# Products of the identity in TensorE's planned pauses, six places for the last loads of u, and another order of the work

## The chip, the cores and the metric

The kernel runs on one core of one Trainium2 chip. The metric is the device time of one execution in microseconds (us). TensorE (PE) multiplies into the eight banks of PSUM, VectorE (DVE) and ScalarE (ACT) empty the banks and do the elementwise work, GpSimd (POOL) does reductions over partitions and some copies, and SyncE (SP) issues nearly all transfers. A multiply of float32 numbers that must keep their accuracy is written as three multiplies of rounded parts (high times high, high times low, low times high).

## The reference

```python
def reference(q, k, v, moe_*, moe2_*):
    # attention: batch 4, 8 heads, 576 tokens, 64 numbers a head; heads 0-3 see a window of 32,
    # heads 4-7 every fourth token of a window of 128
    attn = softmax(where(mask, q @ k.T / 8, -1e9)) @ v          # -> x (4, 576, 512)
    # first feed-forward part: 512 -> 1024 -> 512, gated by a convolution over 3 tokens
    h = relu(x @ w_in); gate = sigmoid(conv3(h, conv_w))
    x = (h * gate) @ w_out
    # second part: Fourier transform over tokens and numbers, real part, then layer norm and 512 -> 2048 -> 512
    u = x + real(fft(fft(x, axis=1), axis=2))
    un = (u - mean(u)) / sqrt(var(u) + 1e-6)
    return u + relu(un @ w_ch1) @ w_ch2
```

## The kernel before

The stages follow one another and overlap: the attention of the four batches (`tick`: scores, maximum, exponential, product with v, transposes; 14 ticks a batch), the first feed-forward part batch by batch (`m1`, `m2`), the Fourier transform as products with tables (`dft`), the layer norm (`ln`), and the second feed-forward part. The last is done first in three `runs` over eight blocks of 128 hidden rows (`n1`, `n2`), and then over the pairs of blocks that are left, for three sets of six token tiles (`pair7`, `down6`; 16 steps k = 0 to 15, the last set of tokens in k = 12 to 15). Its sums stay in six PSUM banks over the steps of a set. At the end of a set `add_up` loads for each tile the residual u from DRAM, adds the bank to it on DVE and stores the result. In the three runs the partial sums go back to DRAM in the same way. The loads of u go to places that a `Ring` hands out in turn. From step k = 7 that ring has four places, so the fifth and the sixth load of a set use the first two again. The weights come in as float64 and are narrowed and split on DVE (`Weights.narrow`: three instructions; `Weights.split`: a subtraction and a copy).

No engine's instructions are written out in the order in which they run. Each piece of work is given to `Plan.add` with its engines, its assumed duration and what it reads and writes. `Plan.urgency` works out a due time (`key`) for each. `NUDGES` is a list of seeds: each seed draws a stretch of due times and moves the due times in it at random by up to 1, 2, 4 or 8 us. `Plan.order` then plays the engines through in planned time and picks, for each engine when it comes free, the ready work of lowest due time. It lists the work in that order, and `Plan.issue` emits the instructions; each engine then runs its own part of the list strictly from the top, waiting for semaphores. The planned times themselves don't reach the chip, only the order does. The plan's duration for a product is that of one clock of TensorE throughout:

```python
        if b.form.dtype == F32R:
            us = max(0.109, 0.014 + 0.000417 * n)
...
        else:
            us = 0.014 + 0.0004 * n
```

The line L270 of the profile is the call of `matmul` or `transpose` in `Plan.products`, L257 that of all elementwise work in `Plan.run`, L299 that of a transfer in `Plan.dma`; L639 and L642 are the normalising of attention on DVE and ACT. The rows that matter here name tiles: `pb` is a PSUM bank, `wf` a pair of weight blocks, `hid` the hidden layer, `x` the tokens of one batch or the place that later holds weights, `rows` a scratch tile of which `cv_t`, `g_t` and `hpad` are parts, `ud` the DRAM copy of u, `raw` the place of incoming float64 weights (later of u and of results), `xb` the normalised attention output before its transpose with `ident`, and `tb` the Fourier tables.

Of the kernel before, what the change touches and what calls it, by code (L numbers as in the profile page):

```python
# [12 lines left out]
F32 = mybir.dt.float32  # L13
# [4 lines left out]
BF16 = mybir.dt.bfloat16  # L18
# [6 lines left out]
DM, FF1, FF2 = 512, 1024, 2048  # L25
# [90 lines left out]
class View:  # L116
# [3 lines left out]
    def __init__(self, tile_, form, ops=()):  # L120
        self.tile, self.form, self.ops = tile_, form, ops
# [65 lines left out]
class Work:  # L187
# [2 lines left out]


NUDGES = (72966, 90854, 53149, 44608, 8896, 40657, 44910, 40292, 90802, 9591, 97362, 78696,
          82639, 89740, 72233, 58905, 68874, 57268, 11083, 9893, 22435, 84083, 88604, 81921,
          11822, 6492, 54663, 30756, 71614, 11936, 95714, 64261, 51939,)


LAT = {"PE": 0.25, "DVE": 0.12, "ACT": 0.15, "POOL": 0.2, "SP": 0.0, "NO": 0.0}
# [5 lines left out]
class Plan:  # L203
    def __init__(self, engines):
        self.engines, self.works, self.key, self.piece = engines, [], 1e9, None
        self.opened = []


    def touch(self, w, view, write):
# [14 lines left out]
        keep.append((w.id, write, box))  # L224
        s.log = keep

    def add(self, where, fn, reads, writes, key=None, nbytes=0, after=()):
        w = Work()
        w.id = len(self.works)
        w.where, w.fn, w.deps, w.bytes, w.after = where, fn, set(after), nbytes, {}  # L230
        w.key = self.key if key is None else key
        self.works.append(w)
        for v in reads:
            self.touch(w, v, False)
        for v in writes:
            self.touch(w, v, True)
        return w

    def run(self, where, op_, key=None, **kw):
# [20 lines left out]
    @contextmanager  # L260
    def products(self, key):

        self.piece = []
        yield self
        todo, self.piece = self.piece, None
        us = sum(t[0] for t in todo)

        def fn(_):
            for _, name, a, kw in todo:
                getattr(self.engines["PE"], name)(*[v.real() for v in a], **kw)  # L270
        self.add({"PE": us}, fn, [v for t in todo for v in t[2][1:]], [t[2][0] for t in todo], key)

    def mm(self, o, a, b, start, stop, more=False):
        n = b.n()
# [35 lines left out]
    def order(self):  # L310
        W = self.works
        for w in W:
            w.succ, w.left, w.ready, w.start = [], len(w.deps), 0.0, None
        for w in W:
            for d in w.deps:
                W[d].succ.append(w.id)
        self.urgency()
        for seed in NUDGES:
            rng = random.Random(seed)
            a = rng.uniform(0, 560)  # L320
            z = a + rng.uniform(4, 50)
            amp = rng.choice((1, 2, 4, 8))
            for w in W:
                if a < w.key < z:
                    w.key += rng.uniform(-amp, amp)
        self.urgency()
        free = dict.fromkeys(("PE", "DVE", "ACT", "POOL", "SP", "NO"), 0.0)
        can = {e: {} for e in free}
        bus, drift = 0.0, 0.0
        out = []  # L330

        def can_wait(w, end):
            return w.key < 1e8 and end < w.key + min(w.where.values()) + drift

        def offer(w):
            for e in w.where:
                can[e][w.id] = w
        for w in W:
            if not w.left:
                offer(w)  # L340
        while any(can.values()):
            best = None
            for e, c in can.items():
                if c:
                    t = max(free[e], min(w.ready for w in c.values()))
                    if best is None or t < best[0]:
                        best = t, e
            t, e = best
            pick = None

            wait = WAIT.get(e, 0.0)
            for w in sorted((w for w in can[e].values() if w.ready <= t + wait + 1e-9), key=lambda w: w.key):
                late = False
                for e2, us in w.where.items():
                    if e2 != e:
                        queue = sum(x.where[e2] for x in can[e2].values()
                                    if x.key < w.key and x.ready <= t and len(x.where) == 1)
                        if max(free[e2], t) + queue + us < t + w.where[e] - 1e-9 and not (
                                us < w.where[e] and can_wait(w, t + w.where[e] + 0.5)):
                            late = True  # L360
                if not late:
                    pick = w
                    break
            if pick is None:

                free[e] = min([f for x, f in free.items() if f > t + 1e-9] + [t + 0.3])
                continue
            w = pick
            for x in w.where:
                del can[x][w.id]  # L370
            t = max(t, w.ready)
            w.start, w.eng = t, e
            if e == "PE":
                drift += 0.1 * (t - w.key - drift)
            end = t + w.where[e]
            free[e] = end
            if w.bytes:
                begin = max(bus, end)
                bus = begin + w.bytes / 265e3
                end = bus + 2.0  # L380
            out.append(w)
            for s in w.succ:
                x = W[s]
                lat = 0.0 if w.bytes else LAT[e] if e not in x.where else 0.0
                x.ready = max(x.ready, end + lat)
                x.left -= 1
                if not x.left:
                    offer(x)
        assert len(out) == len(W), [w.id for w in W if w.start is None][:5]
        return out  # L390

    def issue(self):
# [4 lines left out]
class Pool:  # L397
# [28 lines left out]
    def fill(self, n):  # L426

        if n % LINE:
            self.tile([128, n % LINE // 4], F32, "room")
# [12 lines left out]
def tile_kernel(ctx: ExitStack, tc: tile.TileContext, forms, qt_in, ktp, ktd, vtp, vtd, wm1, wm2, conv_w,  # L442
                tab, mask, ident16_in, ident_in, out):
    nc = tc.nc
    ctx.enter_context(tc.manual_schedule())
    P = Plan({"ACT": nc.scalar, "DVE": nc.vector, "POOL": nc.gpsimd, "PE": nc.tensor, "SP": nc.sync})
# [18 lines left out]
    def dve(op_, us, key=None, **kw):  # L465
        P.run({"DVE": us}, op_, key, **kw)
# [27 lines left out]
    ident = const.tile([128, 128], F32, "ident")  # L494
# [523 lines left out]
    hidden, rings, later_, tmp7, tok = {}, {}, [], [], {}  # L1018
# [115 lines left out]
    def sums7(j, raw, place_):  # L1134

        a, b = (r.bitcast(F32) for r in raw)
        for x, w in ((a, W2.tiles[0, 2 * j]), (b, W2.tiles[0, 2 * j + 1])):
            w = w.bitcast(F32)
            dve("tensor_tensor", on_dve(512), out=x[:, 0:512], in0=w[:, 0], in1=w[:, 1], op=ALU.add)
        x11, x12, s1, s2 = (a[:, 256 * i:256 * i + 256] for i in range(4))  # L1140
        x21, x22, s3, s4 = (b[:, 256 * i:256 * i + 256] for i in range(4))
        for o, x, y, op in ((s1, x21, x22, ALU.add), (s2, s1, x11, ALU.subtract),
                            (s3, x11, x21, ALU.subtract), (s4, x12, s2, ALU.subtract)):
            dve("tensor_tensor", on_dve(256), out=o, in0=x, in1=y, op=op)
        for i, r in enumerate((a, b)):
            o = place_[:, 2 * i:2 * i + 2]
            v = r[:, 512:1024].rearrange("p (i n) -> p i n", i=2)
            copy(o[:, :, 0], v, ("ACT", "POOL"))
            lo_of(o[:, :, 1], v, o[:, :, 0])
# [81 lines left out]
                add_up(SIX[s][t], acc, at + step * (t + 1) / 6, True, 2 if end and t == 5 else 1)  # L1231


    dve("memset", 0.05, out=tiny)
    P.add({"DVE": 0.05}, lambda _: nc.vector.memset(eps.real(), 1e-9), [], [eps], -95)

# [50 lines left out]
    for k in range(2 * NF1):  # L1287
        _, i, f = W1.todo[k]
# [59 lines left out]
    def stage(j):  # L1348
        return comb[:, 7 * (j % 2):7 * (j % 2) + 7]
# [10 lines left out]
    at = T5  # L1360
    for r, (p, _) in enumerate(runs):
        nt = len(SETS[p])
        for f in range(R0):
            step = WHEN["first"][1] if r == 0 else 1.38 * nt
            if r == 0:
                at = WHEN["first"][0] + step * f
            if (r, f) == (1, 0):
                at = T5
# [4 lines left out]
            if (r, f) == (1, 1):  # L1373
# [11 lines left out]
                flat = [g.rearrange("p j l n -> p (j l n)") for g in groups]  # L1385
# [20 lines left out]
    todo = [(0, j) for j in range(R0 // 2)] + [(s, j) for s in range(3) for j in late]  # L1406
    tokens7(0, tok[0])
    free = [r.bitcast(F32)[:, DM * i:DM * i + DM] for r in raws for i in range(2)]
    left = iter(range(R0 + 6, NF2))
    for k, (s, j) in enumerate(todo):  # L1410
        if k == 7:
            rings["u"], rings["o"] = Ring(rings["u"].views[:2] + free[:2]), Ring(rings["o"].views[:2] + free[2:])
        if j == late[1] and s < 2:
            tokens7(s + 1, tok[s + 1])
        hid = hid_t if k % 2 else other[k >= 4]
        pair7(s, j, hid, tok[s], comb, ring, sums, at, STEP)
        if k < 2:
            sums7(k + 2, (few(), few()), part(k))
        for _, f in zip(range(3 if k < 2 else 1), left):
            second7(f, few)  # L1420
        down6(s, j, hid, at + STEP, STEP, bool(j == 0 or s and j == late[0]), j == late[-1], s == 2)
        if 2 <= k < 6:
            weights7(k + 2, few, stage(k))
        at += STEP
# [80 lines left out]
```

## Time and profile before

| | before |
|---|---|
| median of 3 runs | 747.86 us (745.51 to 748.53) |
| time of the profiled execution | 749.69 us |
| its span, first to last instruction | 747.9 us |
| TensorE busy with products | 724.0 us, 97% |
| VectorE busy | 561.5 us, 75% |
| ScalarE, GpSimd busy | 344.4 us, 152.4 us |
| mean granted TensorE clock | 0.982 |

A busy share says how long an engine had an instruction in work; it says nothing on what it waited for in the rest. The granted clock is 1 at 2.4 GHz and 0.5 at 1.2 GHz, and a TensorE at the lower clock is as busy as at the higher one while it does half the work. What a stretch of a stage is worth is therefore read from three things together: TensorE's pauses, its clock, and which engine was working without a pause at that time.

### The profile page before, as it was taken

The page shows a single profiled execution, that of the slowest core. Times are in us where ns is not written, and L with a number is a line of the kernel's source. Part 1 is how long each engine was busy: PE and PEld are TensorE (multiplying, and loading weights), DVE is VectorE, ACT ScalarE, POOL GpSimd, SP SyncE. Part 2 cuts the span into 40 slices and gives each one's busy share as a digit, 9 for nine tenths or more (in the row PEclk, how much of TensorE's full clock was granted, in tenths as well). Part 3 has the DMA queues.
Part 4 walks back from the last instruction along what each step waited for, and adds up shares of the span by engine and source line. Part 5 has one row for each costly group of instructions (what it writes and reads, how often), then busy time and mean ns, then how long its engine had stood idle before and what let it go on. Part 6 is the DMA issues. An engine that isn't in the chain of part 4 may idle for free.

```text
span 747.9 us, 11906 instructions
## 1 busy us (share of the span) xinstructions
PE 724.0 (97%) x4189; PEld 642.6 (86%) x4189; DVE 561.5 (75%) x1189; ACT 344.4 (46%) x891; POOL 152.4 (20%) x168
## 2 busy tenths in 40 slices
PE   7899989999999999998999999999999999999997
PEld 5788879998998999886888888899999889988895
DVE  6889999899989689889788889576878738324223
ACT  4768767766676565463243325233233323222220
POOL 4646514443555112110000100010011000000000
PEclk9869999999999999999899999999999999999999
DMA  9944454323510834686966914133545799648303
GB/s 251 258 130 136 163 152 136 100 74 116 185 51 29 288 131 127 208 273 225 314 236 227 301 46 132 29 140 113 156 156 186 247 351 325 180 118 277 90 1 112
DMA packets 75095, 126.57 MB, mean 169 GB/s; under 512 B 7570, under 2 KB 35986, under 8 KB 74396
## 3 DMA queue, kind: packets, MB, share of 16 engines
q1 hardware_dynamic: 74236, 122.86, 51.9%
q0 software_dynamic: 432, 2.67, 0.9%
q8 instruction: 33, 0.54, 0.3%
q10 hardware_dynamic: 368, 0.28, 0.1%
q14 instruction: 26, 0.21, 0.1%
HBM read 89.85 MB, written 35.94 MB: 168 GB/s over the span
## 4 chain that ended last, share of the span: by engine, by line
PE 80%; DVE 9%; DMA 5%; ACT 3%; POOL 1%; issue 1%; SPq 1%; ACTq 0%; DVEq 0%; POOLq 0%
PE pb L270 80%; DMA maskt<-in_mask_dram 2%; DVE rows L257 2%; POOL mx L257 1%; DMA ud<-y 1%; DVE sm L257 1%; DVE sq L257 1%; DVE wf L257 1%; SPq L299 1%; DVE win L257 1%; DMA KT<-in_ktd_dram 1%; DVE y L257 1%; DMA rows<-ud 1%; DVE hid L257 1%; DVE raw L257 1%
## 5 line engine op out<-in xcount | busy, mean ns | idle before, releaser
L270 PE MATMUL pb<-wf,hid 128*128 128x512 f32 x870 | 230.6, 400 | 2.5 <-DVE hid L257 2.5
L270 PEld LDWEIGHTS pb<-wf,hid 128*128 128x128 f32 x870 | 158.5, 190 | 29.3 <-DVE hid L257 3.0
L270 PE MATMUL pb<-x,wf 128*128 128x288 f32 x768 | 115.7, 301 | 2.1 <-ACT rows L257 1.2
L270 PEld LDWEIGHTS pb<-x,wf 128*128 128x128 f32 x768 | 107.6, 190 | 5.6 <-ACT rows L257 2.1
L257 POOL PARTITION_ALL_REDUCE mx<-sm x56 | 88.0, 1586 | 78.0 <-DVE sm L257 42.4
L270 PE MATMUL pb<-wf,wc 128*128 128x384 f32 (+1 forms) x414 | 85.2, 343 | 0.0
L257 DVE TENSOR_TENSOR work<-pb,work 128x384 f32<-128x384 f32 x48 | 26.7, 556 | 71.1 <-ACT work L257 38.2
L270 PEld LDWEIGHTS pb<-wf,wc 128*128 128x128 f32 x414 | 74.2, 188 | 5.9
L257 ACT COPY work<-pb 128x384 f32<-128x384 f32 x48 | 23.0, 479 | 88.1 <-PE pb L270 88.1
L257 DVE SCALAR_TENSOR_TENSOR rows<-rows,convw 128x576 f32<-128x576 f32 x64 | 54.7, 855 | 4.1 <-ACT rows L257 3.3
L270 PE MATMUL pb<-wf 128*128 128x512 f32 x216 | 55.1, 393 | 0.0
L270 PEld LDWEIGHTS pb<-VT,sm 104*72 104x72 f32 (+1 forms) x448 | 41.9, 162 | 8.4 <-ACT sm L257 4.8
L270 PE MATMUL pb<-VT,sm 104*72 104x65 f32 (+1 forms) x448 | 44.3, 246 | 4.7 <-ACT sm L257 1.9
L642 ACT ACTIVATE xb<-pb,rs 72x64 f32<-72x64 f32 (+1 forms) x196 | 44.4, 306 | 4.3 <-DVE rs L257 4.1
L270 PEld LDWEIGHTS pb<-wf 128*128 128x128 f32 x216 | 40.1, 188 | 6.6
L270 PE MATMUL pb<-QT,KT 128*104 128x144 f32 (+1 forms) x224 | 42.6, 314 | 0.7 <-DMA QT<-in_qt_dram 0.6
L257 ACT ACTIVATE rows<-pb 128x288 f32<-128x288 f32 x64 | 26.3, 411 | 34.4 <-PE pb L270 33.2
L270 PE MATMUL pb<-wf,wf 128*128 128x512 f32 (+1 forms) x162 | 39.9, 386 | 0.0
L270 PEld LDWEIGHTS pb<-QT,KT 128*104 128x104 f32 (+1 forms) x224 | 34.2, 184 | 6.6 <-issue 3.6
L257 DVE TENSOR_TENSOR sm<-sm,mx 104x288 f32<-104x288 f32 (+1 forms) x56 | 33.8, 606 | 7.2 <-POOL mx L257 7.1
L257 ACT ACTIVATE hid<-pb 128x512 fp32r<-128x512 f32 (+1 forms) x32 | 18.3, 572 | 42.7 <-PE pb L270 42.5
L270 PEld LDWEIGHTS pb<-wf,wf 128*128 128x128 f32 x162 | 29.8, 188 | 5.5
(193 smaller groups left out, 1224.2 us busy)
## 6 DMA issues: line engine op xcount, KB each, us to landing
raw<-in_wm_dram SPq DMA_DIRECT2D x42, 512.0 KB, 5.0
wc<-cd SPq DMA_DIRECT2D x56, 256.0 KB, 2.9
cd<-wc SPq DMA_DIRECT2D x4, 1792.0 KB, 10.9
rows<-ud SPq DMA_DIRECT2D x24, 256.0 KB, 2.7
y<-yd SPq DMA_DIRECT2D x18, 256.0 KB, 3.1
ud<-y SPq DMA_DIRECT2D x18, 256.0 KB, 4.6
wf<-nd SPq DMA_DIRECT2D x18, 256.0 KB, 4.2
QT<-in_qt_dram SPq DMA_DIRECT2D x31, 144.0 KB, 3.7
```

The source lines that it names most:

```text
L257: getattr(self.engines[eng], name)(**a)
L270: getattr(self.engines["PE"], name)(*[v.real() for v in a], **kw)
L299: self.engines[eng].dma_start(out=out.real() if outs else out, in_=in_.real() if ins else in_)
L642: nc.scalar.mul(out=x[:, i], in_=p[:, i], mul=r[:, i:i + 1])
```

## The change

There are three parts.

1. `Plan.order` notes when TensorE has been left without work for over 0.4 us of planned time (after the first 8 us of the plan). Ahead of the work that ends such a pause it puts multiplications of the identity: `fill` looks for a bank whose uses so far have all ended in the plan and whose next use begins a new sum, and `busy_with` issues n plain bf16 products of 128 x 128 by 256 columns into it, n so that they end 0.25 us before the planned start of that work, at 0.12 us each. Nothing reads what they write. The plan's own times aren't changed by them.
2. From step k = 12 on the ring for u has six places, in the tile `flat[3]` (weights that were last used in step 3), and that for the results six as well, two of `rows` and four of `raw`.
3. `NUDGES` loses four seeds (81921, 6492, 54663, 71614) and gains 21.

```diff
@@ NUDGES
-          82639, ..., 88604, 81921,
-          11822, 6492, 54663, 30756, 71614, 11936, 95714, 64261, 51939,)
+          82639, ..., 88604, 11822,
+          30756, 11936, 95714, 64261, 51939, 63844, 16121, 48697, 73536, 40816, 51048, 85030,
+          41210, 53495, 13473, 46513, 14900, 32254, 45147, 44590, 28542, 77181, 66469, 2489,
+          13351, 95203,)
@@ Plan.add
+        for t in {v.tile for v in (*reads, *writes) if v.tile.whole}:
+            self.uses.setdefault(t, []).append((w, t in fresh))
@@ Plan.products
+        fresh = {}
+        for _, _, a, kw in todo:
+            fresh.setdefault(a[0].tile, kw.get("start", True))
@@ Plan.order
+        seen = dict.fromkeys(self.uses, (0, 0.0))
+        def fill(t0, t1):
+            free_at = []
+            for tile_, uses in self.uses.items():
+                i, end = seen[tile_]
+                while i < len(uses) and uses[i][0].start is not None:
+                    x = uses[i][0]
+                    i, end = i + 1, max(end, x.start + x.where[x.eng])
+                seen[tile_] = i, end
+                if 0 < i < len(uses) and uses[i][1]:
+                    free_at.append((end, len(free_at), tile_))
+            end, _, tile_ = min(free_at, default=(t1, 0, None))
+            n = int((t1 - max(t0, end) - 0.25) / 0.12)
+            return self.busy_with(tile_, max(t0, end), n) if n > 0 else []
...
             if e == "PE":
+                if 8.0 < t and t - last > 0.4 and self.busy_with:
+                    out += fill(last, t)
+                last = t + w.where[e]
@@ tile_kernel
+    def busy_with(tile_, at, n):
+        w = Work()
+        w.where, w.eng, w.start, w.bytes, w.deps, w.key, w.ready, w.id = {"PE": 0.12 * n}, "PE", at, 0, set(), at, at, -1
+        def fn(_):
+            x = ident.real().bitcast(BF16)
+            for _ in range(n):
+                nc.tensor.matmul(tile_.real[:, 0:256], x[:, 0:128], x, start=True, stop=True)
+        w.fn = fn
+        return [w]
+    P.busy_with = busy_with
@@ the steps of the last part
+        if k == 12:
+            rings["u"] = Ring([flat[3].bitcast(F32)[:, DM * i:DM * i + DM] for i in range(6)])
+            rings["o"] = Ring(rings["o"].views[:2] + free)
```

## Rows read from the trace of the kernel before

**Rows 1.** The page: busy times, and the chain that ended last by engine.
```profile
PE 724.0 (97%) x4189; PEld 642.6 (86%) x4189; DVE 561.5 (75%) x1189; ACT 344.4 (46%) x891; POOL 152.4 (20%) x168
...
PE 80%; DVE 9%; DMA 5%; ACT 3%; POOL 1%; issue 1%; SPq 1%; ACTq 0%; DVEq 0%; POOLq 0%
```

**Rows 2.** Busy time by stretch: stretch, length, engines, granted clock, DMA share, GB/s.
```profile
0.00:8.00 8.00, 6.03 (x23) 3.21 (x24) 4.70 (x15) 1.87 (x3) 0.95 (x6) 1.00 0.77 209
8.00:58.00 50.00, 42.49 (x318) 39.08 (x317) 40.47 (x91) 36.18 (x125) 29.62 (x23) 0.83 0.78 211
58.00:108.00 50.00, 46.76 (x343) 42.30 (x343) 47.78 (x92) 36.92 (x110) 23.05 (x22) 1.00 0.51 156
108.00:300.00 192.00, 190.96 (x1320) 175.18 (x1319) 170.21 (x361) 125.42 (x360) 77.68 (x88) 1.00 0.38 123
300.00:348.00 48.00, 46.59 (x256) 39.87 (x256) 43.12 (x111) 23.40 (x48) 6.18 (x10) 1.00 0.72 239
348.00:353.50 5.50, 1.98 (x13) 1.21 (x11) 5.43 (x13) 2.88 (x5) 0.91 (x1) 0.92 0.67 184
353.50:742.80 389.30, 389.24 (x1925) 341.70 (x1925) 249.02 (x510) 117.78 (x244) 14.05 (x21) 0.99 0.55 179
742.80:747.90 5.10, 0.00 (x0) 0.00 (x0) 0.75 (x2) 0.00 (x0) 0.00 (x0) 0.73 0.45 167
```

**Rows 3.** The same columns for the stretches around the lower clock.
```profile
13.00:17.60 4.60, 2.48 (x24) 1.99 (x23) 3.15 (x9) 3.96 (x16) 3.12 (x3) 1.00 1.03 288
18.50:21.70 3.20, 3.20 (x20) 3.19 (x19) 1.98 (x4) 1.62 (x5) 2.31 (x2) 0.53 1.04 244
33.00:35.40 2.40, 0.97 (x9) 0.55 (x7) 2.25 (x8) 1.66 (x9) 0.33 (x1) 0.94 0.98 292
35.40:40.40 5.00, 2.90 (x21) 2.54 (x21) 4.33 (x16) 3.49 (x14) 2.83 (x2) 0.50 0.83 235
40.40:48.70 8.30, 7.72 (x37) 7.34 (x37) 6.37 (x12) 5.02 (x17) 4.32 (x3) 0.50 0.37 113
...
352.20:359.70 7.50, 6.23 (x15) 4.94 (x16) 7.13 (x14) 1.46 (x3) 0.00 (x0) 0.54 1.01 291
```

**Rows 4.** The chain that ended last, from 352 us: start, length, what.
```profile
353.47 385.20 PE pb L270 x1907
...
738.69 0.70 DVE rows L257
...
739.79 4.18 DMA rows<-ud
```

**Rows 5.** DVE's timeline at the end; in brackets, the idle before and its releaser.
```profile
740.05 0.69 DVE L257 TENSOR_TENSOR raw<-raw,pb 128x512 f32<-128x512 f32 x1 [0.67 <-PE pb L270]
741.41 0.69 DVE L257 TENSOR_TENSOR rows<-rows,pb 128x512 f32<-128x512 f32 x1 [0.67 <-PE pb L270]
744.17 0.75 DVE L257 TENSOR_TENSOR rows<-rows,pb 128x256 f32<-128x256 f32 x2 [2.07 <-DMA rows<-ud]
```

**Rows 6.** TensorE's timeline: a plain bf16 product at the higher clock, and its successor.
```profile
6.88 0.33 PE L270 MATMUL pb<-maskt,ident 128*128 128x384 bf16 x1
7.04 0.81 PE L270 MATMUL pb<-QT,KT 128*128 128x192 f32 x4
```

**Rows 7.** TensorE's timeline: work that ended a pause, the first, a middle and last.
```profile
13.74 0.89 PE L270 MATMUL pb<-VT,sm 128*96 128x65 f32 x8 [0.51 <-ACT sm L257]
...
35.76 0.50 PE L270 MATMUL pb<-ident,xb 72*128 72x72 f32 x2 [0.68 <-ACT xb L642]
...
353.47 4.64 PE L270 MATMUL pb<-wf,hid 128*128 128x512 f32 x10 [2.51 <-DVE hid L257]
```

**Rows 8.** Timeline after the long pause: the last weights' split, and their first product.
```profile
358.72 0.68 DVE L257 TENSOR_TENSOR x<-rows,x 128x512 fp32r<-128x512 f32 x1
359.69 0.69 DVE L257 TENSOR_TENSOR x<-rows,x 128x512 fp32r<-128x512 f32 x1 [0.29 <-ACT x L257]
...
361.36 1.52 PE L270 MATMUL pb<-x,hid 128*128 128x512 f32 x6
```

More of the change, by code (lines that the diff above doesn't have):

```diff
@@ L192 @@
 NUDGES = (72966, 90854, 53149, 44608, 8896, 40657, 44910, 40292, 90802, 9591, 97362, 78696,
-          82639, 89740, 72233, 58905, 68874, 57268, 11083, 9893, 22435, 84083, 88604, 81921,
-          11822, 6492, 54663, 30756, 71614, 11936, 95714, 64261, 51939,)
[4 rows of a table added]
 LAT = {"PE": 0.25, "DVE": 0.12, "ACT": 0.15, "POOL": 0.2, "SP": 0.0, "NO": 0.0}
@@ L206, in __init__ @@
         self.opened = []
+        self.uses, self.busy_with = {}, None
     def touch(self, w, view, write):
@@ L225, in touch, with add @@
         s.log = keep
-    def add(self, where, fn, reads, writes, key=None, nbytes=0, after=()):
+    def add(self, where, fn, reads, writes, key=None, nbytes=0, after=(), fresh=()):
         w = Work()
@@ L270, in fn @@
                 getattr(self.engines["PE"], name)(*[v.real() for v in a], **kw)
-        self.add({"PE": us}, fn, [v for t in todo for v in t[2][1:]], [t[2][0] for t in todo], key)
+        fresh = {}
+        for _, _, a, kw in todo:
+            fresh.setdefault(a[0].tile, kw.get("start", True))
+        self.add({"PE": us}, fn, [v for t in todo for v in t[2][1:]], [t[2][0] for t in todo], key,
+                 fresh=[t for t, new in fresh.items() if new])
     def mm(self, o, a, b, start, stop, more=False):
@@ L328, in order @@
         can = {e: {} for e in free}
-        bus, drift = 0.0, 0.0
+        bus, drift, last = 0.0, 0.0, 0.0
         out = []
+        seen = dict.fromkeys(self.uses, (0, 0.0))
[12 more added lines that the diff above has]
+            return self.busy_with(tile_, max(t0, end), n) if n > 0 else []
         def can_wait(w, end):
@@ L388, in order @@
                     offer(x)
-        assert len(out) == len(W), [w.id for w in W if w.start is None][:5]
+        assert all(w.start is not None for w in W), [w.id for w in W if w.start is None][:5]
         return out
```

1 row of the table NUDGES is left out of this document.

## The prediction

> **What bounds the kernel now.** I read the page first [rows 1]: TensorE is busy 97% and makes up 80% of the chain that ended last. A share of 97% leaves little to fill, so the next question is where the rest lies. The table by stretches [rows 2] answers it. From 353.5 to 742.8 us TensorE has no pause at all (389.24 of 389.30 us): half of the run is bound by TensorE alone, at 2.4 GHz but for its first six microseconds. Before that it pauses for 2.0 us until 8 us, 7.5 us from 8 to 58, 3.2 us from 58 to 108, 1.0 us from 108 to 300, 1.4 us from 300 to 348 and 3.5 us from 348 to 353.5; then there are 5.1 us at the end. In the three stretches with pauses after 58 us VectorE has no room: 47.78 of 50, 43.12 of 48, 5.43 of 5.5 us. So there VectorE sets the pace, and between them TensorE does.
>
> The same table with narrower stretches shows the second loss [rows 3]. Three times TensorE ran at 1.2 GHz: for 3.2 us from 18.5, for 13.3 us from 35.4 and for 7.5 us from 352.2. Each time it had been broken up before: busy for 2.48 of 4.60 us ahead of the first, 0.97 of 2.40 ahead of the second, and the longest pause of the run (2.51 us [rows 7]) led into the third. The work in these stretches is 3.20, 2.90 + 7.72 and 6.23 us; at 2.4 GHz it takes half, so the whole price of the lower clock is (3.20 + 10.62 + 6.23) / 2 = 10.0 us, of which 6.9 us lie before 50 us. Whether it is paid at the end is another matter. Up to 40 us the DMA share is 0.83 to 1.04: transfers, not TensorE, set the pace there.
>
> Last, the chain from 352 us on [rows 4]: one unbroken piece of TensorE to 738.7, then an addition on DVE, then a load of u of 4.18 us that could be issued only when that addition had read the place it goes to.
>
> **The change part by part.**
>
> **Six places for u.** The additions of the last set start 1.36 us apart (740.05, 741.41), each when TensorE has finished its bank; the sixth starts at 744.17, after 2.07 us of idle time that ended with the load [rows 5]. With a place of its own its load doesn't wait for an addition, and the tile that it goes to was last read hundreds of microseconds earlier. The addition then starts at 741.41 + 1.36 = 742.77, **1.40 us** earlier, and the two stores behind it move with it. The loads are the same six in number and bytes, so nothing is added to the queue; issued earlier, they lie beside 389 us without a pause of TensorE. Bounds: -1.4 us if nothing else moves, 0 if the six loads are issued as late as now. I take -1.4, since the row shows exactly one cause.
>
> **The filling, its price.** A plain product of 384 bf16 columns is followed 0.16 us later by the next [rows 6]: 0.417 ns a column, so 256 columns take 0.107 us, and 0.213 us at half the clock. How many there will be depends on the plan's pauses, which no row shows; as an estimate I take the trace's own. After 8 us and before the last product there are 18 pauses over 0.4 us, 14.9 us in all, the first of 0.51 and the last of 2.51 us [rows 7]. By the rule of the change (length less 0.25, over 0.12, rounded down) they hold 78 products, 8.3 us at full clock. In a real pause they cost nothing; TensorE waits anyway. Where the plan has a pause and the chip none, they cost their full length. Bounds: 0 and +8.3 us. The plan's durations know one clock; the chip's TensorE is late by up to 6.9 us early on, which shifts all later work with it, so most pauses should still be there. I take +1.0, an eighth. The weights of these products are loaded from the identity, which came in with the first transfers, and the bank chosen is the one longest free, so I take no new wait from them.
>
> **The filling, the clock before 50 us.** If the pauses around 13 to 17 and 33 to 40 us are filled but for some 0.3 us each, TensorE is busy for roughly three quarters of these stretches in place of 2.48 of 4.60 and 0.97 of 2.40 us, and it has stayed at 2.4 GHz through 58 to 108 us with pauses like these. Bounds: 0 and -6.9 us. Of this the first 1.6 us and the part to 40.4 us (1.5 us) lie under full transfer queues. The 7.72 us after 40.4 are the part that can count: 3.9 us. VectorE is busy 6.37 of 8.30 us there, so it can follow by at most 1.9 us before it is the bound, and it stays the bound to 108 us. I take **-1.8**.
>
> [...]
>
> **The filling, the clock after 352 us.** The six microseconds of work would take 3.1 us less, and after them TensorE doesn't pause again, so what is won is kept. But VectorE is busy 7.13 of 7.50 us, and the weights whose first product starts at 361.36 are ready at 360.38 [rows 8]: with the order unchanged TensorE could be 0.98 us earlier and no more. Bounds: 0 and -3.1. I take **-1.2**, near the row.
>
> **The new order.** Drawn from the seeds themselves, the added ones move due times from 48 to 423 us of the plan, eight of them within 86 to 140; the removed ones moved 38 to 80 and 187 to 210. It neither adds nor takes away work. What it can win is at most the pauses after 58 us, 3.2 + 1.0 + 1.4 + 3.5 = 9.1 us [rows 2]. VectorE has 22 us to spare from 108 to 300, so a weight conversion put off from before 108 would give room. Losing is as easy: another crowding of VectorE like that at 348 costs 3.5 us, two cost 7. Bounds: -9.1 and +7. I take **-2.5**, a good quarter of what is there, between the ends and nearer to the pauses that exist than to those that would have to appear.
>
> **Sum.** -1.4 + 1.0 - 1.8 - 1.2 - 2.5 = -5.9 us. Against the profiled execution (749.69 us, of which 747.9 are the span and 1.8 lie around it) that is 743.8. The median of the three runs is 747.86, 1.83 lower; there the sum gives **742.0 us**, -0.8%. Differences of up to 0.5% (3.7 us) are what a measurement here can't tell from none.
>
> **The rivals.**
>
> *Everything meets.* The order closes the pauses of VectorE's stretches and the clock holds: -1.4 - 3.5 - 3.1 - 6 = -14, 734 us. For it speaks that these are the places where pauses lie; against it, that VectorE is busy over 90% in each, so its work must go elsewhere, not only in another order.
>
> *VectorE takes it back.* TensorE gains before 50 and after 352 us, and waits for VectorE instead; only the end is left: 747.86 - 1.4 = 746.5. VectorE's 47.78 of 50 us speak for it, its spare 22 us later against it.
>
> *The clock falls anyway.* The quarter of a microsecond left open in each pause, or pauses in other places than planned, leave TensorE as broken up as before. Then the two clock terms vanish and 742.0 + 3.0 = 745.0 remain. For it speaks that TensorE was still busy over half of the time ahead of the first fall; against it, the 2.4 GHz held through 58 to 108 us.
>
> *The filling stands in the way* (slower). TensorE comes to the products after their pause has passed, and ready work queues behind them, with what waits for its banks on ACT and DVE. If all 78 meet no pause: +8.3 - 1.4 = +6.9, 754.8 us. At 13 products (1.4 / 0.107) the gain of the end is gone if nothing else is won, at 48 the kernel is slower by over 0.5%. For it: TensorE runs up to 6.9 us behind a plan that knows one clock. Against it: the pauses are waits for ACT, DVE and transfers, which move along with TensorE.
> The Trainium skill (TensorE: Matmul & The Clock Gate, Part 3, "What overlaps and what doesn't") has matmuls start and end strictly in program order; no row here shows one overtaking another, and by this rule such a filling can't be passed.
>
> **How the numbers follow.** The forecast, 738 to 745 us, gets 0.40; everything meets 0.15; VectorE takes it back 0.16; the clock falls anyway 0.15; the filling stands in the way 0.14. Faster by over 0.5% is below 744.1 us: 0.37 of the first case, all 0.15 of the second, 0.03 of the fourth: 0.55. Slower by over 0.5%, above 751.6: 0.12, nearly all of the last. The rest, 0.33, is in between. For 8 in 10 the range starts at 735 (a third of the second case is left out below) and ends at 750 (0.13 above).
>
> **What would show it.** After the change the sixth addition follows the fifth by about 1.4 us and no load of u lies in the chain's end. Bf16 products of 256 columns stand in TensorE's timeline between 8 and 360 us, about 78. The granted clock is 1.00 at 18 to 22 and 40 to 49 us and after the pause near 350. TensorE's pauses after 58 us add up to about 6.5 us. The prediction is wrong if the filling lengthens stretches that had no pause, if VectorE's crowded stretches grow, or if pauses appear after 353 us.

## The result, and the profile after

The changed kernel takes 740.63 us (median of 7 runs, 738.23 to 743.23) beside 747.39 us of the kernel before (7 runs, 745.51 to 748.57): a ratio of 0.9907, 95% interval 0.9883 to 0.9931, or 6.9 us less, give or take 1.8. Run again for the experiments, beside 18 runs of the kernel before, it gave 739.00 and 0.9889 (0.9866 to 0.9913). The forecast was 742.0 us in 735 to 750, and faster.

Busy times, granted clock by slices of a fortieth of the span, and the chain that ended last by engine, from the page of the changed kernel:

```profile
PE 728.4 (98%) x4312; PEld 647.8 (88%) x4312; DVE 557.1 (75%) x1187; ACT 350.1 (47%) x903; POOL 148.0 (20%) x158
...
PEclk9989999999999999999999999999999999999999
...
PE 86%; DMA 6%; DVE 5%; ACT 1%; POOL 1%; SPq 0%; issue 0%; ACTq 0%; DVEq 0%; POOLq 0%
```

TensorE has 123 products more and its share rose, although the kernel computes nothing more; the products of the identity count as busy. So the first line of this page has become useless as a measure of how well TensorE is used. The table by stretches, in the columns of [rows 2], and the group of the new products by shape:

```profile
8.00:58.00 50.00, 45.95 (x392) 42.20 (x390) 42.49 (x95) 38.12 (x132) 31.46 (x24) 0.93 0.85 228
58.00:108.00 50.00, 48.95 (x361) 44.53 (x360) 47.22 (x92) 37.53 (x112) 23.12 (x20) 1.00 0.47 147
108.00:300.00 192.00, 191.22 (x1331) 176.37 (x1329) 170.28 (x375) 126.83 (x357) 74.65 (x84) 1.00 0.40 130
300.00:348.00 48.00, 48.00 (x286) 41.26 (x286) 43.33 (x104) 26.23 (x52) 5.84 (x10) 1.00 0.70 232
348.00:353.50 5.50, 5.50 (x26) 4.57 (x25) 5.43 (x11) 2.03 (x4) 0.00 (x0) 1.00 0.97 281
353.50:736.00 382.50, 382.41 (x1907) 335.88 (x1905) 242.90 (x499) 117.62 (x246) 12.31 (x17) 1.00 0.54 178
736.00:739.90 3.90, 0.12 (x1) 0.00 (x0) 0.75 (x2) 0.00 (x0) 0.00 (x0) 0.94 0.37 134
```

```profile
L1271 PE MATMUL pb<-ident 128*128 128x256 bf16 x123 | 17.3, 285 | 0.0
```

Three things differ from [rows 2 and 3]. The clock is 0.93 in place of 0.83 from 8 to 58 us, and 1.00 from 300 to 736 us; the 5.50 us from 348 are full where TensorE was busy for 1.98. The last stretch, behind TensorE's last products, is 3.9 us long where it was 5.1. VectorE's additions at the end:

```profile
734.80 0.69 DVE L262 TENSOR_TENSOR raw<-wf,pb 128x512 f32<-128x512 f32 x1 [0.67 <-PE pb L275]
736.16 0.75 DVE L262 TENSOR_TENSOR raw<-wf,pb 128x256 f32<-128x256 f32 x2 [0.67 <-PE pb L275]
```

The sixth follows the fifth by 1.36 us and waits for TensorE alone; in [rows 5] it followed by 2.76 and waited for its load.

### The profile page after: what moved, and what is told of

Its sections match the earlier page's. It is cut to its first block, busy times and chain, and to the rows that moved or that the text cites. A ratio compares the mean times of both kernels' runs of the same rounds, so it can differ in the third digit from the quotient of the medians.

```text
span 739.9 us, 12155 instructions
## 1 busy us (share of the span) xinstructions
PE 728.4 (98%) x4312; PEld 647.8 (88%) x4312; DVE 557.1 (75%) x1187; ACT 350.1 (47%) x903; POOL 148.0 (20%) x158
## 4 chain that ended last, share of the span: by engine, by line
PE 86%; DMA 6%; DVE 5%; ACT 1%; POOL 1%; SPq 0%; issue 0%; ACTq 0%; DVEq 0%; POOLq 0%
PE pb L275 85%; DMA raw<-in_wm_dram 3%; DMA QT<-in_qt_dram 2%; DVE win L262 1%; PE pb L1271 1%; POOL mx L262 1%; DMA maskt<-in_mask_dram 1%; DVE sm L262 1%; DVE raw L262 1%; DVE rows L262 0%; SPq L308 0%; DVE wc L262 0%; DVE hid L262 0%; DVE fo L262 0%; DVE x L262 0%
## 5 line engine op out<-in xcount | busy, mean ns | idle before, releaser
L275 PE MATMUL pb<-x,wf 128*128 128x288 f32 x768 | 113.9, 298 | 0.5 <-ACT rows L262 0.5
L275 PEld LDWEIGHTS pb<-x,wf 128*128 128x128 f32 x768 | 106.0, 188 | 3.4 <-ACT rows L262 1.2
L262 POOL PARTITION_ALL_REDUCE mx<-sm x56 | 90.7, 1638 | 59.7 <-ACT sm L262 24.5
L262 DVE SCALAR_TENSOR_TENSOR rows<-rows,convw 128x576 f32<-128x576 f32 x64 | 58.2, 909 | 4.3 <-ACT rows L262 3.8
L275 PEld LDWEIGHTS pb<-VT,sm 104*72 104x72 f32 (+1 forms) x448 | 40.2, 156 | 6.5 <-issue 2.8
L275 PE MATMUL pb<-VT,sm 104*72 104x65 f32 (+1 forms) x448 | 41.6, 239 | 3.0 <-DVE x L262 2.5
L262 DVE TENSOR_TENSOR sm<-sm,mx 104x288 f32<-104x288 f32 (+1 forms) x56 | 31.2, 561 | 6.9 <-POOL mx L262 6.7
L262 POOL CAST wc<-raw 128x512 fp32r<-128x512 f32 (+1 forms) x10 | 7.2, 718 | 138.4 <-PE pb L275 48.2
```

The costliest lines, as they stand in the source:

```text
L262: getattr(self.engines[eng], name)(**a)
```

## The experiments

Eleven kernels ran, each timed in five rounds beside the kernel before, in three groups; those of a group share a chip. The ratio is to the kernel before.

| run | filling | places | seeds | median us | ratio, 95% interval |
|---|---|---|---|---|---|
| order_alone | none | old | new | 747.09 | 1.0003 (0.9984 to 1.0021) |
| fill_alone | all | old | old | 743.58 | 0.9944 (0.9926 to 0.9962) |
| places_alone | none | six | old | 744.76 | 0.9981 (0.9964 to 0.9998) |
| no_fill | none | six | new | 745.27 | 0.9975 (0.9957 to 0.9993) |
| front_only | 50 early products | six | new | 740.48 | 0.9921 (0.9893 to 0.9949) |
| late_only | 73 late products | six | new | 743.97 | 0.9959 (0.9942 to 0.9977) |
| shorter | 36 for 45 near 340 us | six | new | 739.26 | 0.9899 (0.9876 to 0.9922) |
| shorter_front | that, and 28 for 6 near 33 us | six | new | 741.01 | 0.9923 (0.9895 to 0.9950) |
| changed_again | all | six | new | 739.00 | 0.9889 (0.9866 to 0.9913) |
| old_seeds | all | six | old | 743.33 | 0.9929 (0.9903 to 0.9954) |
| twice | each twice as long | six | new | 746.88 | 1.0004 (0.9988 to 1.0021) |

**The parts by themselves.** `order_alone`, `places_alone` and `no_fill` leave out the filling, `order_alone` and `fill_alone` the six places; `fill_alone` and `places_alone` have the old seeds.

```diff
-    P.busy_with = busy_with                  # order_alone, places_alone, no_fill
-        if k == 12:                          # order_alone, fill_alone
-            rings["u"] = Ring([...])
-            rings["o"] = Ring(rings["o"].views[:2] + free)
-NUDGES = (the new seeds)                     # fill_alone, places_alone
+NUDGES = (the old seeds)
```

Expected of `order_alone`:

> The new seeds alone, without the products of the identity and without the six places. Theory (the gain is the clock that the filling holds, plus the end): the pauses remain and the clock still falls near 36 and near 340 us, so this is within 2 us of the kernel before, 745 to 749 us. Rival (the new order is what gains): 741 to 744 us, and TensorE's pauses after 58 us are shorter by several us than the 9.1 us of the kernel before.

Of `fill_alone`:

> The filling alone, with the old seeds and the old places. Theory (clock): 741.5 to 743.5 us, with the granted clock at 1.00 after the pause near 350 and a shorter lower stretch before 50 us; the sixth addition still waits for its load. Rival (order): within 2 us of the kernel before, as the filling stands partly in the way of ready work.

Of `places_alone`:

> The six places alone. Theory: 1.4 us less than the kernel before, the sixth addition 1.36 us after the fifth, nothing else moved. Rival: the six loads, issued earlier, delay weights in the last part and TensorE gets a pause after 353 us, so nothing is won.

Of `no_fill`:

> The changed kernel without its products of the identity. Theory (clock): the clock falls for some 13 us before 50 us and for 6 to 8 us after the pause near 340; 5 to 7 us more than the changed kernel, 745 to 748 us. Rival (order): within 2 us of the changed kernel, 739 to 743 us.

Measured: the new order alone +0.2 us (give or take 1.4), the filling alone -4.2 (1.3), the places alone -1.4 (1.3), order and places together -1.9 (1.3). The times are those of the theory (743.58 us of `fill_alone` lie a little above its 741.5 to 743.5); of the clock that it expected in `fill_alone`, one part failed, as shown below. The order by itself is worth nothing that can be seen. Between `no_fill` and the changed kernel the ratio falls from 0.9975 to 0.9907, 5.1 us (2.2) for the filling. The stretches of `no_fill` at the lower clock, in the columns of [rows 3]:

```profile
35.20:45.60 10.40, 8.66 (x46) 8.14 (x47) 9.34 (x21) 5.91 (x20) 4.65 (x3) 0.52 0.56 172
...
342.80:346.90 4.10, 4.08 (x13) 2.76 (x12) 3.27 (x7) 0.64 (x2) 0.00 (x0) 0.59 0.78 213
```

At the lower clock TensorE works without a pause for most of the time (8.66 of 10.40, 4.08 of 4.10 us): it is slow there more than waiting.

The executions of one and the same program point the same way. `no_fill` was executed 12 times; each result has the span and the mean granted clock. The slowest took 748.46 us at 0.982, the fastest 741.20 at 0.993. Time at 1.2 GHz is twice (1 - clock) times the span, so it is 26.9 and 10.4 us in these two. A straight line through the 12 has 0.39 us of span for each us at 1.2 GHz (correlation 0.93); the three other programs that lack all or part of the filling and were executed 12 times give 0.48 (`places_alone`, correlation 0.98), 0.35 (`order_alone`, 0.89) and 0.30 (`late_only`, 0.65). Half a microsecond would be the price if all of it were work of TensorE that the end waits for. The line alone doesn't show the clock as the cause: a load that lands late makes a pause longer and can cost the clock behind it as well (the pause near 33 us below). The medians of the time at 1.2 GHz are 19 us in `no_fill` and 3.0 us in the changed kernel; at 0.39 that is 6 us, about the measured difference.

The second fall of the clock survived in `fill_alone`. TensorE's timeline there, and the stretch behind it in the columns of [rows 2]:

```profile
351.64 4.04 PE L273 MATMUL pb<-wf,hid 128*128 128x512 f32 x10 [2.41 <-DVE hid L260]
```

```profile
351.64:355.00 3.36, 3.36 (x8) 2.69 (x9) 3.29 (x6) 0.70 (x1) 0.00 (x0) 0.52 1.04 308
```

This is the long pause of [rows 7], 2.41 us for 2.51, with no product of the identity in it, so the plan of the old seeds has no pause there that it would fill.

**The two halves of the filling.**

```diff
+        if at > 60:            # front_only; late_only: if at < 60
+            return []
```

Expected of `front_only`:

> The changed kernel with only the 50 products of the identity that the plan puts before its 60 us; the 73 later ones are left out. Theory (each half of the filling pays for its own stretch of lower clock): against the kernel with the new order and places but no filling, about 2.5 us less; the clock still falls near 343 us; 742 to 744 us. Rival (only the long filling near 340 us pays): as without filling, 745 us.

Of `late_only`:

> The changed kernel with only the 73 later products of the identity. Theory (each half pays for its own stretch): the clock is 1.00 after 340 us, the lower stretch before 50 us is as long as without filling; 2 to 2.5 us less than without filling, 742.5 to 744 us. Rival (only the front pays, since the 45 products near 340 us hold up the transposes behind them by 1 us): 744.5 to 745.5 us.

Measured against `no_fill`: the front 0.9921 / 0.9975, -4.0 us (2.5), the late part 0.9959 / 0.9975, -1.2 (1.9). The two add up to the whole, -5.1, and the front pays. Of the late part the times don't show that it pays: its interval reaches beyond 0. They don't show either that the front is worth more than the 2.5 us of the theory and the late part less, though both medians lie that way; the rows further down say more.

**The size of the filling.** `shorter` cuts the longest one, `shorter_front` lengthens one of the front besides, `twice` doubles all.

```diff
+        n = 36 if n == 45 else n                          # shorter
+        n = 36 if n == 45 else 28 if n == 6 else n        # shorter_front
+        n = 2 * n                                         # twice
```

Expected of `shorter`:

> The changed kernel with 36 instead of 45 products in the pause near 340 us. Theory (the last nine stand in the way of transposes that are ready): the transposes start 1.0 us earlier, the clock stays at 1.00, and the time is 0.5 to 1.0 us less, 739.5 to 740 us. Rival (the transposes are not what the following work waits for): no difference.

Of `shorter_front`:

> As the one before, and 28 instead of 6 products in the pause near 33 us, which is 2.5 us longer on the chip than in the plan. Theory (the clock falls at 36 us because that pause is filled too little): the clock stays at 1.00 through 36 to 43 us, 1 to 2.5 us less than with the shorter filling alone, 737.5 to 739 us. Rival (up to 40 us the transfers set the pace, or VectorE takes it back): the clock holds and the time stays within 0.7 us of the one before.

Of `changed_again`, the changed kernel once more, for comparison:

> The changed kernel once more, beside the next two on one chip: 0.7% to 1.1% less than the kernel before, as before.

Of `twice`:

> The changed kernel with each filling twice as long: 246 products of the identity in place of 123. The added 123 last 13.2 us at 0.107 us each. Theory (an overlong filling stands in the way of ready work wherever no pause is left, and work after it can't pass): 6 to 13 us more than the changed kernel. Rival (most of the added products fall into time that TensorE would wait anyway, or is given back later): 0 to 3 us more.

First the long filling near 340 us. TensorE and ACT in the changed kernel, where `y<-y,sq` on ACT ends the layer norm of two tiles and TensorE transposes them:

```profile
337.36 5.09 PE L1271 MATMUL pb<-ident 128*128 128x256 bf16 x45
...
340.39 1.52 ACT L262 ACTIVATE y<-y,sq 128x512 f32<-128x512 f32 x2 [0.51 <-DVE sq L262]
...
342.28 1.04 PE L275 MATMUL pb<-ident,y 128*128 128x128 f32 x8
...
344.56 1.55 PE L275 MATMUL pb<-wf,wf 128*128 128x512 f32 x6
```

In `no_fill`:

```profile
340.71 1.52 ACT L262 ACTIVATE y<-y,sq 128x512 f32<-128x512 f32 x2 [0.50 <-DVE sq L262]
341.57 1.39 PE L275 MATMUL pb<-ident,y 128*128 128x128 f32 x8 [3.78 <-ACT y L262]
...
345.71 0.62 PE L275 MATMUL pb<-wf,wf 128*128 128x512 f32 x1
```

In `shorter`:

```profile
336.75 1.52 ACT L262 ACTIVATE y<-y,sq 128x512 f32<-128x512 f32 x2 [0.50 <-DVE sq L262]
337.66 1.31 PE L275 MATMUL pb<-ident,y 128*128 128x128 f32 x8
...
339.87 1.20 PE L275 MATMUL pb<-wf,hid 128*128 128x512 f32 x4 [0.43 <-DVE hid L262]
340.91 1.53 PE L275 MATMUL pb<-wf,wf 128*128 128x512 f32 x6
```

Without filling the transposes start 0.86 us after ACT. With 45 products they start 1.89 after it, so the filling holds them up by 1.03 us; with 36 they start 0.91 after it. Yet the next block of products with `wf` follows ACT by 4.17 us with 45, by 4.16 with 36, and by 5.00 with none: what the shorter filling wins, TensorE spends waiting for `hid` from VectorE. So by these rows the nine products cost nothing, and the rival of that run is favoured. The times (0.9899 beside 0.9889 and 0.9907) fit it, but with some 2.5 us either way they can't tell nothing from the 0.5 to 1.0 us of the theory. The rows also give a reason why the late half may be worth so little: VectorE sets the pace there, and between these two executions the higher clock wins 5.00 - 4.17 = 0.83 us at this place, not 2.

Twice as much, 90 products, is another matter. The same place in `twice`:

```profile
336.94 10.00 PE L1272 MATMUL pb<-ident 128*128 128x256 bf16 x90
...
339.67 1.52 ACT L262 ACTIVATE y<-y,sq 128x512 f32<-128x512 f32 x2 [0.51 <-DVE sq L262]
...
346.78 1.04 PE L275 MATMUL pb<-ident,y 128*128 128x128 f32 x8
```

The transposes start 7.11 us after ACT. Against `changed_again` on the same chip the ratio is 1.0004 / 0.9889, +8.6 us (2.2): of the added 123 products, 13.2 us long, most stood in the way, and the clock of 1.00 throughout doesn't help. The Trainium skill (TensorE: Matmul & The Clock Gate, Part 3, "What overlaps and what doesn't") has matmuls start and end in program order; these rows agree, since transposes ready near 340.5 us stood behind the filling until 346.78.

Then the pause near 33 us. The filling, VectorE's work beside it and the work behind it in the changed kernel, in `changed_again` and in `shorter_front`:

```profile
33.15 0.82 PE L1271 MATMUL pb<-ident 128*128 128x256 bf16 x6
...
34.28 0.43 DVE L262 TENSOR_SCALAR win<-raw 128x512 int32<-128x512 int32 x1 [1.66 <-DMA raw<-in_wm_dram]
...
36.51 2.16 PE L275 MATMUL pb<-VT,sm 104*72 104x65 f32 x16 [2.54 <-DVE x L262]
```

```profile
31.91 0.43 DVE L262 TENSOR_SCALAR win<-raw 128x512 int32<-128x512 int32 x1 [0.25 <-DMA raw<-in_wm_dram]
...
32.18 0.82 PE L1271 MATMUL pb<-ident 128*128 128x256 bf16 x6
33.53 1.22 PE L275 MATMUL pb<-VT,sm 104*72 104x65 f32 x16 [0.53 <-ACT sm L262]
```

```profile
33.41 3.22 PE L1272 MATMUL pb<-ident 128*128 128x256 bf16 x28
...
34.87 1.05 DVE L262 TENSOR_TENSOR x<-pb,x 128x144 fp32r<-128x144 f32 x3
...
36.47 1.20 PE L275 MATMUL pb<-VT,sm 104*72 104x65 f32 x16
```

The first two are the same program. The pause behind the six products is 2.54 us in one execution and 0.53 in the other, and only in the first does the clock fall after it: the products with `VT` take 2.16 us there and 1.22 in the other. In the first VectorE stood 1.66 us for a load of `raw` just before, in the other 0.25. In `shorter_front` the clock held at 1.00 with a filling 2.40 us longer, 3.22 for 0.82. In the good case, which has 0.53 us of pause left behind the six products, it would be some 1.9 us too long, and in its own execution it was too long as well: the products with `VT` start 0.55 us after VectorE begins on `x` in both others (35.96 and 32.98 us), and 1.60 us after it here, so they stood 1.05 us behind the filling. The ratio, 0.9923, is no better than that of `shorter`, 0.9899: 1.8 us more, give or take 2.7. My theory for it, 1 to 2.5 us less, fell. The rival, the clock holds and the time stays within 0.7 us, is neither shown nor excluded, and it didn't have the 1.05 us.

**The seeds under the filling.**

```diff
-NUDGES = (the new seeds)
+NUDGES = (the old seeds)
```

Expected of `old_seeds`:

> The changed kernel with the old seeds: filling and six places, no new order. Theory (filling and places are the whole gain): within 1.5 us of the changed kernel beside it; TensorE's clock still falls near 350 us, where the plan of the old seeds has no pause. Rival (the new order adds to the filling by moving that pause to where the plan sees it): 2 us or more above the changed kernel.

Measured 0.9929 beside 0.9889, 3.0 us (2.6) more than the changed kernel. The rival is favoured, just outside the noise: the new order seems to be worth something with the filling that it isn't worth alone. Its reason was only half seen. In the profile of `old_seeds` the pause of 2.4 us on `hid` is there, unfilled, but the clock didn't fall after it in that execution (1.00 from 349.84 to 355 us).

That makes it a measure of what the clock is worth there. `places_alone` has the same seeds and places and no filling, of which the plan of `old_seeds` has none behind 325 us, and its clock fell behind the same pause (0.56 from 350.20 to 357 us). TensorE behind the pause and VectorE's sixth addition, first in `old_seeds`, then in `places_alone`:

```profile
349.84 2.56 PE L273 MATMUL pb<-wf,hid 128*128 128x512 f32 x10 [2.39 <-DVE hid L260]
...
362.53 1.07 PE L273 MATMUL pb<-tb,fl 128*128 128x290 f32 x6 [1.70 <-DVE AT L260]
...
738.26 0.75 DVE L260 TENSOR_TENSOR raw<-wf,pb 128x256 f32<-128x256 f32 x2 [0.67 <-PE pb L273]
```

```profile
350.20 4.64 PE L273 MATMUL pb<-wf,hid 128*128 128x512 f32 x10 [2.54 <-DVE hid L260]
...
739.45 0.75 DVE L260 TENSOR_TENSOR raw<-wf,pb 128x256 f32<-128x256 f32 x2 [0.67 <-PE pb L273]
```

From the block behind the pause to the sixth addition 388.42 us pass in the first and 389.25 in the second. Between these two executions the higher clock won 0.83 us, and TensorE, ahead by more at first, gave part of it back in a pause of 1.70 us for VectorE.

## Why the prediction was right, and which of its terms were not

**The sum** held: -5.9 us forecast, -6.9 (1.8) measured, and -8.3 (1.8) in `changed_again`. It held in part by luck, since the term of the order, as a gain of its own, was too large and the one of the clock before 50 us too small.

**Six places**, -1.4 us: measured -1.4 (1.3) alone, and the rows show the mechanism to the hundredth, 2.76 - 1.36 = 1.40 us at the end of the chain.

**The number of products**, 78 by the trace's own pauses: 123. The old plan holds 70 (counted in `fill_alone` and `old_seeds`), so the old trace was a fair measure of the old plan. The difference is mostly one pause of the new plan near 340 us with 45 of them, which it could not show. **Their price**, +1.0 us: the rows show 1.03 us of hold-up at that place, and none of it is left at the next block of `wf`. What would make them costly was sized rightly: doubled, 13.2 us of products cost 8.6.

**The clock before 50 us** is the term that was too small: -1.8 forecast, the front half of the filling measured at -4.0 (2.5) with its own price in it. That interval still holds 1.8; what goes beyond it are the rows, of one execution each. The step that failed is "it can follow by at most 1.9 us before it is the bound, and it stays the bound to 108 us". The stretch of `changed_again`, where the clock held, and the same block of TensorE's timeline in three executions, with VectorE's first work behind the load near 33 us:

```profile
8.00:58.00 50.00, 48.63 (x425) 44.15 (x425) 45.62 (x104) 41.90 (x146) 33.36 (x25) 1.00 0.82 232
```

`changed_again` (its load is shown above, 31.91):

```profile
99.50 1.87 PE L275 MATMUL pb<-x,wf 128*128 128x288 f32 x12 [0.43 <-ACT rows L262]
```

`front_only`:

```profile
33.20 0.43 DVE L262 TENSOR_SCALAR win<-raw 128x512 int32<-128x512 int32 x1 [1.29 <-DMA raw<-in_wm_dram]
...
101.52 1.86 PE L275 MATMUL pb<-x,wf 128*128 128x288 f32 x12 [1.06 <-ACT rows L262]
```

`no_fill`:

```profile
33.32 0.43 DVE L262 TENSOR_SCALAR win<-raw 128x512 int32<-128x512 int32 x1 [1.74 <-DMA raw<-in_wm_dram]
...
104.67 1.87 PE L275 MATMUL pb<-x,wf 128*128 128x288 f32 x12 [0.46 <-ACT rows L262]
```

VectorE did 45.62 us of work between 8 and 58 us, against 40.47 in [rows 2]: its idle time of the whole stretch, not only of 40.4 to 48.7 us, was there to be used. The block comes 5.17 us earlier in `changed_again` than in `no_fill`, but 1.41 us of that the load had already brought (31.91 beside 33.32). `front_only` is the better pair: there the load came at 33.20, nearly as in `no_fill`, and the block is 3.15 us ahead, more than the 1.9 that the step allowed. The other traces with the new seeds agree: without the front filling the block comes at 104.49 and 105.49 (`order_alone`, `late_only`), with it at 100.69 and 101.74 in `shorter` and `shorter_front`, where the clock held, and only at 104.34 in the page of the changed kernel, where it fell at 36 us. From this block to the start of `y<-y,sq` near 340 us 236.02 to 236.06 us pass in seven of these eight traces (237.27 in `shorter_front`), so what is ahead at 100 us is, but for that one, still ahead at 340. The rival *VectorE takes it back* failed here.

**The clock after 352 us**, -1.2 forecast, -1.2 (1.9) for the late half, so the times don't show it. The rows do, and for the reason given, that VectorE's work and not TensorE's clock ends this stretch: 0.83 us near 340 us in the new plan, and 0.83 us behind the long pause of the old one, near the 0.98 that the prediction read from [rows 8]. The prediction's sign against it, pauses after 353 us, appeared too. TensorE in `changed_again`:

```profile
407.96 0.66 PE L275 MATMUL pb<-ident,work 128*128 128x128 f32 x4 [1.10 <-ACT work L262]
```

The same pause stands in `no_fill` (1.11 us) and not in the page of the changed kernel, so it differs by execution and the filling isn't shown to bring it.

**The new order**, -2.5 forecast as a term of its own: +0.2 (1.4) alone. As a gain of its own this term failed. The added seeds hardly shortened the pauses; without the filling TensorE still waits there, for one 3.78 us in a piece. With the filling the order seems to win 3.0 (2.6). A pause that stands where the plan puts it can be filled, and the one of [rows 7] could not be; that may explain part, but in the execution profiled of `old_seeds` no clock was lost by it, so what the rest consists of stays open.

**The filling stands in the way** and **the clock falls anyway**: each was seen in an experiment (`twice`; the second fall of `fill_alone`), neither decided the changed kernel. In the execution of the changed kernel shown above the clock still fell at 36 us. In the rival *everything meets* the last 6 us of the sum have no row of their own, and VectorE is busy 89.8% (43.12 of 48 us) in one of the three stretches that it calls over 90%; the forecast rests on neither.

## What to carry to other kernels

Look at the granted clock by stretch before trusting a busy share: here TensorE was 97% busy, and the lower clock alone had a price of up to 10.0 us, more than the 9.1 us of pauses that an order could still close. Dummy products are worth placing only where the pause is certain and its length known, for they can't be passed; one sized for the short pause of a good execution lost the clock in a bad one, one sized for the bad one won nothing, and double the length cost more than the whole gain. When two parts of a change are summed, each should be tried alone: the order that looked like the largest term was worth nothing without the filling.

## What the runs showed of the hardware

One program's executions differ by up to 7 us, and go with the time that TensorE spends at 1.2 GHz (748.46 us at a mean clock of 0.982, 741.20 at 0.993, the two extremes of `no_fill`). One source of such differences was seen in the changed kernel: a pause near 33 us, behind a load, is 0.53 us long in one execution and 2.54 in another. With the clock at 0.999 or 1.000 in each of its six timed executions, `changed_again` spreads over 3.4 us (737.96 to 741.33), and `shorter_front`, at the same clock in all six, over 5.4 (739.46 to 744.88). So the clock isn't the only source of the spread, and that holding it makes the time more even isn't shown.
